# A weight matrix split into high and low halves by whole pieces, and the order of issue that goes with it

## The chip, the cores and the metric

The kernel runs on one core of a Trainium2 chip. The metric is the device time of one execution in microseconds (us). Five engines work in parallel, each on a queue of its own: TensorE (PE, matmuls, with PEld for the loads of its weights), VectorE (DVE), ScalarE (ACT), GpSimd (POOL) and SyncE (SP), which issues the DMAs. An engine takes the instructions of its queue in order; one that waits holds up all behind it.

## The reference

Three stages follow each other, in fp32: attention, an MLP with a leaky rectifier, and a gated MLP with an rms norm. The change is in the second, whose input x has 2304 rows (tokens) and whose weights are w_in[512, 2048] and w_out[2048, 512].

```python
def _moe_ref(x, w_in, w_out, alpha):
    h = x @ w_in
    g = np.maximum(h, 0.0) + alpha * np.minimum(h, 0.0)
    return (g @ w_out).astype(np.float32)

# around it: x is the attention's output (4 batches, 8 heads, 576 positions of 64:
# a softmax over a sequence averaged by 4, plus a softmax over |i - j| < 4), and
# the result goes through silu(n @ w_gate) * (n @ w_val) @ w_out2, n = rms norm of it
```

## The kernel before

TensorE multiplies 16-bit floats. To keep fp32 accuracy, each operand is split in two 16-bit halves, hi and lo, and a product is three matmuls (hi hi, hi lo, lo hi). The helper `split` does it in two instructions: ACT writes hi = f16(s * src), and DVE writes lo = f16(s * src - hi).

w_in comes from HBM in six pieces `p1`, of 384 columns each (the last of 128), since a piece fits in one tile: `load` issues the DMAs, `decode` turns the raw words (`wr`) into fp32 (`wc`) with ACT and DVE (L1186, L1189, L1191, L1194, L1195), and `square` sums squares on PE (`sqps`, L1207, read by DVE in L1208), from which a scale `swi` per piece is made (L430). Then `split_in` fills the tile `wi`, which holds both halves for 16 groups f of 128 hidden columns (each f: 512 numbers per partition and half, four blocks of 128 for the four slices of the contraction). It is called once per f, so three times for a piece.

`m1_first` is the first pass over x, in three chunks c of 192 tokens each. For c = 0 it goes over f in pairs: `split_in(f)`, `split_in(f + 1)`, then `h_mm`. `h_mm` makes 24 matmuls into a PSUM tile `hps` (L1432), ACT reads it with Relu into `g` (L1436), DVE adds the two sides of the rectifier in `hps` (L1438, one for each f), and `split` makes the halves of g (L439, L440; named `g` or `ghl`). The pool of `hps` has two buffers: a third pair must wait for the read-out of the first. `o_mm` (L1449) multiplies with w_out into `acc`. Around these, slots of other work are woven in: the attention of the next chunk (`lsps`, `dls`, `sps`, `dd`, `atps`, `lops`), and the pieces of later weights. The later weights `w`, among them those of the gated MLP, are split by whole pieces of 1536 numbers per partition. The gated MLP's own matmuls are those of L1684 (`pa`, `pb`, `pf`), read out by ACT in L1689 (`sn`), and its results leave through `ob`.

The order in which all these stand in the queues isn't that of the code. `issue_order` builds the graph of dependences, gives every instruction a duration from a formula, and schedules the list by "leads": the instruction with the largest lead that is ready goes first. It then adds a table `LEADS` of triples (from, to, shift), which shifts the lead of instructions by their number in the program; the queues that come out are fixed by added dependences. One instruction more or less in the program shifts the numbers behind it.

Of the kernel before, what the change touches and what calls it, by code (L numbers as in the profile page):

```python
# [18 lines left out]
def view(ap, dims, off=0, parts=None):  # L19
# [2 lines left out]


LEADS = (
# [43 lines left out]
)  # L68


# [249 lines left out]
def kernel(  # L320
# [14 lines left out]
    nc = tc.nc  # L335
    B, H, S, D = q.shape
    DM, FF = w_in.shape
    FF2 = w_gate.shape[1]
    KK = DM // 128
# [55 lines left out]
    wi = wts.tile([128, NF, 2, KK * 128], F16, name="wi")  # L395
# [3 lines left out]
    def col(i):  # L399
        return sc[:, i:i + 1]  # L400
# [37 lines left out]
    def split(hi, lo, src, s):  # L438
        nc.scalar.activation(out=hi, in_=src, func=AF.Copy, scale=s)  # L439
        nc.vector.scalar_tensor_tensor(out=lo, in0=src, scalar=s, in1=hi, op0=ALU.mult, op1=ALU.subtract)  # L440
# [686 lines left out]
    UC = 384  # L1127
    UW = KK * UC
# [3 lines left out]
    swi = const.tile([128, NP], F32, name="swi")  # L1132
# [78 lines left out]
    p1 = [Piece(w_in, f"u{i}", c0=i * UC, n=min(UC, FF - i * UC)) for i in range(6)]  # L1211
# [47 lines left out]
    def gcol(i, g):  # L1259
        return grp[:, i * NG + g:i * NG + g + 1]  # L1260
# [3 lines left out]
    def scale_out(g):  # L1264
# [12 lines left out]
        if g == NG - 1:  # L1277
# [3 lines left out]
            nc.vector.tensor_scalar(out=grp[:, 0:NG], in0=grp[:, 3 * NG:4 * NG], scalar1=col(S_WO),  # L1281
                                    scalar2=col(S_AL), op0=ALU.mult, op1=ALU.mult)

    def split_in(f):
        p = p1[f // 3]
        o = (f % 3) * 128
        c = p.cv()[:, :, o:o + 128]
        w = wi[:, f].rearrange("p a (k c) -> p a k c", k=KK)
        split(w[:, 0], w[:, 1], c, swi[:, f // 3:f // 3 + 1])

    def wo_f(f):
# [133 lines left out]
    def h_mm(x, f, c0, n, hl, first=False):  # L1425
        fs = hl.shape[1]
        ps = ps_w.tile([128, fs, n], F32, tag="w", name="hps")
        for j in range(fs):
            i = 0
            for kk in range(KK):  # L1430
                for a, b_ in ((0, 0), (0, 1), (1, 0)):
                    nc.tensor.matmul(ps[:, j], wi[:, f + j, a, kk * 128:(kk + 1) * 128], x[:, b_, kk, c0:c0 + n],  # L1432
                                     start=(i == 0), stop=(i == 3 * KK - 1))
                    i += 1
        g = wk.tile([128, fs, n], F32, tag="mm", name="g")
        nc.scalar.activation(out=g, in_=ps, func=AF.Relu, scale=-1.0)  # L1436
        for j in range(fs):
            nc.vector.scalar_tensor_tensor(out=ps[:, j], in0=g[:, j], scalar=oma[:, f + j:f + j + 1], in1=ps[:, j],  # L1438
                                           op0=ALU.mult, op1=ALU.add)
        if first or GF[f] == GF[f + fs - 1]:  # L1440
            split(hl[:, :, 0], hl[:, :, 1], ps, col(S_AL) if first else gcol(0, GF[f]))
            return
        for j in range(fs):
            split(hl[:, j, 0], hl[:, j, 1], ps[:, j], gcol(0, GF[f + j]))
# [53 lines left out]
    def m1_first(slots):  # L1498
# [12 lines left out]
        for c in range(3):  # L1511
            for f in range(0, NF, 2):
                if c == 0:
                    split_in(f)
                    split_in(f + 1)
                h_mm(xt(c // 2), f, c % 2 * CW, CW, hl(c, f, 2), True)
                slots[c](f, NF)
                slots[c](f + 1, NF)
# [513 lines left out]
    for i, (x, n) in enumerate(((al, NF), (rg, KK))):  # L2032
        ps = ps_t.tile([128, n], F32, tag="at", name="vecps")
# [98 lines left out]
```

## Time and profile before

| | |
|---|---|
| median of 3 runs | 911.7 us (911.51 to 911.85) |
| profiled execution | 912.48 us, of which the span 910.8 us |
| granted clock of PE, mean | 0.996 |
| PE busy | 885.3 us (97%) |
| DVE busy | 729.8 us (80%) |
| ACT busy | 570.0 us (63%) |
| POOL busy | 401.8 us (44%) |

The span runs from the first to the last instruction of the profiled execution; the 1.68 us around it are start and end. Busy time is the time in which an engine's instructions ran. A share over the whole span hides that stages differ: where PE has gaps is read in windows.

### The profile page before, as it was taken

To read this page: it belongs to the slowest core of one execution; us is meant where nothing else is said; L and a number is where in the kernel's file an instruction comes from. 1 tells how busy PE (TensorE), PEld (TensorE's weight loads), DVE (VectorE), ACT (ScalarE), POOL (GpSimd) and SP (SyncE) were. 2 spreads that over 40 slices of the span, in tenths; PEclk is the share of its full clock that TensorE was granted. 3 is DMA by queue.
4 is the path that set the end of the run, shared out by engine and by line. 5 is a ranking of instruction groups with operands and counts; after the bars stand their busy time and mean duration, and the time that the engine had idled before them with its cause. 6 is when DMAs were issued, how large, how long until landed. Compare 5 with 4: busy or idle time off the path is not lost.

```text
span 910.8 us, 16778 instructions
## 1 busy us (share of the span) xinstructions
PE 885.3 (97%) x6394; PEld 592.8 (65%) x6394; DVE 729.8 (80%) x1358; ACT 570.0 (63%) x1332; POOL 401.8 (44%) x314
## 2 busy tenths in 40 slices
PE   7987999999999999999999999999999999999997
PEld 5766877799866666666666656654566644556686
DVE  4789987799898788798789789999899891288772
ACT  5999986255763366765796688983366641356730
POOL 1100204999899999496201233211623100268630
PEclk9998999999999999999999999999999999999999
DMA  9976351174333141340630002220000001100001
GB/s 224 297 261 209 104 182 28 53 234 142 106 89 99 44 95 53 102 139 1 195 87 32 1 1 81 94 70 35 24 13 1 1 1 39 32 1 1 1 19 53
DMA packets 54111, 73.81 MB, mean 81 GB/s; under 512 B 22202, under 2 KB 35918, under 8 KB 54030
## 3 DMA queue, kind: packets, MB, share of 16 engines
q1 hardware_dynamic: 54030, 72.74, 26.7%
q8 instruction: 50, 0.82, 0.4%
q14 instruction: 31, 0.25, 0.1%
HBM read 68.01 MB, written 4.72 MB: 80 GB/s over the span
## 4 chain that ended last, share of the span: by engine, by line
PE 85%; ACT 6%; DVE 3%; DMA 2%; POOL 2%; issue 1%; SPq 0%; DVEq 0%; POOLq 0%; ACTq 0%
PE hps L1432 18%; PE acc L1449 17%; PE pa L1684 14%; PE oacc L1807 10%; PE pf L1684 7%; PE pb L1684 3%; PE px L1927 3%; POOL prod L599 1%; PE py L1927 1%; PE lsps L956 1%; PE tps L868 1%; ACT wr L1186 1%; PE lops L1012 1%; ACT wi L439 1%; PE ltps L1000 1%
## 5 line engine op out<-in xcount | busy, mean ns | idle before, releaser
L1432 PE MATMUL hps<-xt,wi 128*128 128x192 f16 (+1 forms) x1536 | 326.8, 290 | 4.6 <-DVE g L440 3.1
L1449 PE MATMUL acc<-ghl,wo 128*128 128x384 f16 (+1 forms) x960 | 231.0, 310 | 0.0
L1432 PEld LDWEIGHTS <-wi 128*128 128x128 f16 x1536 | 148.6, 100 | 57.1 <-issue 6.5
L1449 PEld LDWEIGHTS <-wo 128*128 128x128 f16 x1344 | 128.4, 98 | 56.7 <-issue 0.8
L545 POOL TENSOR_TENSOR prod<-cq,ckv 128x896 f32<-128x896 f32 x48 | 105.5, 2197 | 41.4 <-DVE hps L1438 35.3
L1684 PEld LDWEIGHTS <-ws 128*128 128x128 f16 x864 | 85.0, 99 | 56.7 <-issue 2.7
L599 POOL TENSOR_TENSOR prod<-ls,ckv 128x896 f32<-128x896 f32 x48 | 91.3, 1903 | 9.8 <-DVE lo L612 6.5
L1807 PE MATMUL oacc<-wi,wo 128*128 128x512 f16 x360 | 95.4, 379 | 0.2 <-ACT ob L1811 0.2
L1684 PEld LDWEIGHTS <-w 128*128 128x128 f16 x648 | 63.8, 99 | 41.6 <-issue 0.5
L1436 ACT ACTIVATE g<-hps 128x384 f32<-128x384 f32 x96 | 47.2, 492 | 61.5 <-PE hps L1432 60.9
L1438 DVE SCALAR_TENSOR_TENSOR hps<-g,oma,hps 128x192 f32<-128x192 f32 (+1 forms) x128 | 65.7, 515 | 18.3 <-ACT g L1436 17.3
L1449 PE MATMUL acc<-g,wo 128*128 128x384 f16 (+1 forms) x384 | 70.3, 286 | 0.1
L1664 POOL TENSOR_TENSOR ws<-w 128x768 f32<-128x768 f16 x12 | 22.1, 1852 | 106.8 <-DVE ws L1571 40.8
L1684 PE MATMUL pa<-x,w 128*128 128x384 f16 x216 | 67.1, 326 | 0.1
L1684 PE MATMUL pb<-x,w 128*128 128x384 f16 x216 | 66.2, 326 | 0.0
L1807 PEld LDWEIGHTS <-wo 128*128 128x128 f16 x360 | 35.3, 98 | 41.8 <-issue 0.5
L439 ACT ACTIVATE ghl<-hps,grp 128x384 f16<-128x384 f32 (+1 forms) x73 | 42.2, 578 | 31.9 <-DVE hps L1438 27.2
L612 DVE TENSOR_REDUCE lo<-prod 128x128 f32<-128x896 f32 x48 | 51.7, 1079 | 9.5 <-POOL prod L599 9.2
L1692 DVE TENSOR_TENSOR sn<-pf,sn 128x384 f32<-128x384 f32 x45 | 24.8, 552 | 42.6 <-ACT sn L1689 36.5
L556 DVE TENSOR_REDUCE ls<-prod 128x14 f32<-128x896 f32 x48 | 51.7, 1078 | 4.6 <-POOL prod L545 4.5
L1689 ACT ACTIVATE sn<-pa 128x384 f32<-128x384 f32 x66 | 31.9, 489 | 32.9 <-PE pa L1684 32.7
L1876 POOL TENSOR_TENSOR wr<-wi 128x512 f32<-128x512 f16 x12 | 15.1, 1261 | 84.1 <-DMA out_dram<-ob 77.5
(365 smaller groups left out, 2122.6 us busy)
## 6 DMA issues: line engine op xcount, KB each, us to landing
wr<-in_moe_w_out_dram SPq DMA_DIRECT2D x18, 512.0 KB
wr<-in_moe_w_in_dram SPq DMA_DIRECT2D x10, 768.0 KB
wr<-in_moe_w_gate_dram SPq DMA_DIRECT2D x8, 768.0 KB
wr<-in_moe_w_val_dram SPq DMA_DIRECT2D x8, 768.0 KB
ckv<-in_k_dram SPq DMA_DIRECT2D x7, 768.0 KB
ckv<-in_v_dram SPq DMA_DIRECT2D x7, 768.0 KB
wr<-in_moe_w_out_dram SPq DMA_DIRECT2D x20, 256.0 KB
out_dram<-ob SPq DMA_DIRECT2D x14, 256.0 KB
```

The costliest lines, as they stand in the source:

```text
L439: nc.scalar.activation(out=hi, in_=src, func=AF.Copy, scale=s)
L545: engs[i].tensor_tensor(out=pr, in0=view(st["q"][:, j, t:t + TP], [[D, TP], [0, ND], [1, D]]), in1=view(st["k"][:, j, t:t + TP], [[D, TP], ...
L556: nc.vector.tensor_reduce(out=st["s"][:, j, t:t + TP], in_=st.pop(("p", i)), axis=AX.X, op=ALU.add)
L599: engs[i].tensor_tensor(out=over(pr, i), in0=view(st["s"][:, j, t:t + TP], [[ND, TP], [1, ND], [0, D]]), in1=view(st["v"][:, j, t:t + TP], ...
L612: nc.vector.tensor_reduce(out=st["o"][:, t:t + TP, j], in_=view(pr, [[ND * D, TP], [ND, D], [1, ND]]), axis=AX.X, op=ALU.add)
L1432: nc.tensor.matmul(ps[:, j], wi[:, f + j, a, kk * 128:(kk + 1) * 128], x[:, b_, kk, c0:c0 + n], start=(i == 0), stop=(i == 3 * KK - 1))
L1436: nc.scalar.activation(out=g, in_=ps, func=AF.Relu, scale=-1.0)
L1438: nc.vector.scalar_tensor_tensor(out=ps[:, j], in0=g[:, j], scalar=oma[:, f + j:f + j + 1], in1=ps[:, j], op0=ALU.mult, op1=ALU.add)
L1449: nc.tensor.matmul(acc[e], wo_f(f)[:, a, e * 128:(e + 1) * 128], hl[:, b_], start=(f == f0 and i == 0), stop=(f == f1 and i == 2))
L1684: nc.tensor.matmul(ps, w[:, a, kk, c:c + 128], x[:, b_, kk], start=(start and n == 0), stop=(n == 3 * K2 - 1), skip_group_check=True)
L1807: nc.tensor.matmul(acc, uhl(f)[:, h, a, tt * 128:(tt + 1) * 128], w[:, b_, f % 3], start=(f == fs[0] and i == 0), stop=(f == fs[-1] and i ...
L1927: nc.tensor.matmul(ps, two(u[g])[:, a, tt * 128:(tt + 1) * 128], w(g, b_), start=(start and g == 0 and i == 0), stop=(g == F2 - 1 and i == 2),
```

## The change

w_in's halves are laid out by piece instead of by f: in the tile `wi` a piece has first all its hi numbers, then all its lo numbers, in the order of the decoded piece, so that one `split` can write a whole piece. `split_in` does that for f = 3, 6, 9 and 12 (1536 numbers per partition) and f = 15 (512, the last piece); for the other f above 2 it returns at once. f = 0, 1 and 2 are still split one by one, into the new layout. So 16 splits become 8, on ACT and on DVE. The matmuls read their weights through `wi_w`, again 128 columns in a row.

The program has 16 instructions less behind the splits, and the table of shifts is new: 1,385 triples in place of 212, which moves instructions in the queues of all engines.

```diff
 LEADS = (
-    (8102, 8103, 7000), (776, 777, -500), (3486, 3544, 1500), (7335, 7386, 500), (5591, 5593, -500),
...
 )
...
+    def wi_n(f):
+        return min(UC, FF - f // 3 * UC)
+
+    def wi_p(f):
+        o = f // 3 * 2 * UW
+        return wi.rearrange("p f a c -> p (f a c)")[:, o:o + 2 * KK * wi_n(f)].rearrange("p (a c) -> p a c", a=2)
+
+    def wi_w(f, a, kk):
+        o = kk * wi_n(f) + f % 3 * 128
+        return wi_p(f)[:, a, o:o + 128]
+
     def split_in(f):
+        if f > 2:
+            if f % 3 == 0:
+                w = wi_p(f)
+                split(w[:, 0], w[:, 1], p1[f // 3].c[:, 0:KK * wi_n(f)], swi[:, f // 3:f // 3 + 1])
+            return
         p = p1[f // 3]
         o = (f % 3) * 128
         c = p.cv()[:, :, o:o + 128]
-        w = wi[:, f].rearrange("p a (k c) -> p a k c", k=KK)
+        w = wi_p(f).rearrange("p a (k c) -> p a k c", k=KK)[:, :, :, o:o + 128]
         split(w[:, 0], w[:, 1], c, swi[:, f // 3:f // 3 + 1])
...
-                    nc.tensor.matmul(ps[:, j], wi[:, f + j, a, kk * 128:(kk + 1) * 128], x[:, b_, kk, c0:c0 + n],
+                    nc.tensor.matmul(ps[:, j], wi_w(f + j, a, kk), x[:, b_, kk, c0:c0 + n],
                                      start=(i == 0), stop=(i == 3 * KK - 1))
```

The order in the queues, at three places. Line numbers of after are 234 higher up to the helpers and 250 higher behind them: L673 and L674 are the two lines of `split`, L1686 and L1688 the read-out of `hps`, L1420 to L1429 the decode. First ACT's queue where the splits of `wi` begin, before:

```order
L439 ACTIVATE wi<-wc,swi 128x512 x5
L1186 ACTIVATE wr<-wr 128x768
L439 ACTIVATE wi<-wc,swi 128x512
L1189 ACTIVATE wr<-wr,nhalf 128x768
L1186 ACTIVATE wr<-wr 128x768
L439 ACTIVATE wi<-wc,swi 128x512 x2
L1436 ACTIVATE g<-hps 128x384
```

and after (128x4x128 are f = 0, 1 and 2 in this order, 128x1536 pieces 1 and 2):

```order
L673 ACTIVATE wi<-wc,swi 128x4x128
L673 ACTIVATE wi<-wc,swi 128x1536
L673 ACTIVATE wi<-wc,swi 128x4x128
L1420 ACTIVATE wr<-wr 128x768
L673 ACTIVATE wi<-wc,swi 128x1536
L1423 ACTIVATE wr<-wr,nhalf 128x768
L1420 ACTIVATE wr<-wr 128x768 x2
L1420 ACTIVATE wr<-wr 128x256
L1423 ACTIVATE wr<-wr,nhalf 128x768
L673 ACTIVATE wi<-wc,swi 128x4x128
```

Piece 1 now stands between f = 0 and f = 1, and f = 2 behind piece 2 and five steps of decode.

DVE's queue from the splits of `wi` to the first read-out of `hps`, before:

```order
L440 SCALAR_TENSOR_TENSOR wi<-wc,swi,wi 128x512 x4
L1195 SCALAR_TENSOR_TENSOR wc<-wr,wc 128x768
L440 SCALAR_TENSOR_TENSOR wi<-wc,swi,wi 128x512 x2
L1191 SCALAR_TENSOR_TENSOR wo<-wr 128x768
L1194 TENSOR_SCALAR wc<-wr 128x768
L440 SCALAR_TENSOR_TENSOR wi<-wc,swi,wi 128x512
L1195 SCALAR_TENSOR_TENSOR wc<-wr,wc 128x768
L1438 SCALAR_TENSOR_TENSOR hps<-g,oma,hps 128x192
L440 SCALAR_TENSOR_TENSOR wi<-wc,swi,wi 128x512
L1438 SCALAR_TENSOR_TENSOR hps<-g,oma,hps 128x192 x2
```

and after, from just ahead of the first read-out on (the 128x4x128 here is f = 2, `g_835` the halves of the first pairs):

```order
L1429 SCALAR_TENSOR_TENSOR wc<-wr,wc 128x768
L1429 SCALAR_TENSOR_TENSOR wc<-wr,wc 128x256
L1688 SCALAR_TENSOR_TENSOR hps<-g,oma,hps 128x192
L674 SCALAR_TENSOR_TENSOR wi<-wc,swi,wi 128x4x128
L1442 SCALAR_TENSOR_TENSOR sqps,s_111<-sqps,ident 128x128
L1688 SCALAR_TENSOR_TENSOR hps<-g,oma,hps 128x192
L1425 SCALAR_TENSOR_TENSOR wo<-wr 128x768
L1428 TENSOR_SCALAR wc<-wr 128x256
L674 SCALAR_TENSOR_TENSOR g_835<-hps,sc,g_835 128x2x192
```

The split of f = 2 moved from ahead of the first read-out to between its two steps.

ACT's queue at the first table load of the gated MLP (`sn`, `wi`, `uhl` and `wo` are here results read out of `pa`), before:

```order
L1200 ACTIVATE w_7141,s_115<-wc 128x1536
L1689 ACTIVATE sn<-pa 128x384
L1563 ACT_TABLE_LOAD
L1563 ACTIVATE th<-sn,gsc 128x384
L1689 ACTIVATE sn<-pa 128x384
L1473 ACTIVATE wi<-acc_6158,inv_106 128x192 x2
L1563 ACTIVATE th<-wi,gsc 128x384
L1689 ACTIVATE wo<-pa 128x384
```

and after:

```order
L1434 ACTIVATE w_7125,s_115<-wc 128x1536
L1939 ACTIVATE sn<-pa 128x384
L1939 ACTIVATE uhl<-pa 128x384
L1813 ACT_TABLE_LOAD
L1813 ACTIVATE th<-sn,gsc 128x384
L1939 ACTIVATE sn<-pa 128x384
L1939 ACTIVATE wo<-pa 128x384
```

`uhl` moved behind the sum of squares and so directly ahead of the load; the two steps of L1473 behind the second `sn` moved away.

## Rows read from the trace of the kernel before

**Rows 1.** The page: busy time of the engines, and the chain of work by engine.
```profile
PE 885.3 (97%) x6394; PEld 592.8 (65%) x6394; DVE 729.8 (80%) x1358; ACT 570.0 (63%) x1332; POOL 401.8 (44%) x314
...
PE 85%; ACT 6%; DVE 3%; DMA 2%; POOL 2%; issue 1%; SPq 0%; DVEq 0%; POOLq 0%; ACTq 0%
```

**Rows 2.** Windows of PE: start:end, length, busy (instructions), granted clock, DMA share, GB/s.
```profile
100.00:850.00 750.00, 746.27 (x5234) 1.00 0.21 65
850.00:911.00 61.00, 55.09 (x464) 0.99 0.08 27
```

**Rows 3.** Windows: length, busy of PE, PEld, DVE, ACT, POOL; clock, DMA share, GB/s.
```profile
60.00:70.00 10.00, 6.58 (x60) 5.54 (x61) 9.67 (x17) 9.67 (x16) 0.00 (x0) 1.00 0.93 337
70.00:80.00 10.00, 8.44 (x90) 7.59 (x90) 8.96 (x28) 10.00 (x25) 0.00 (x0) 0.83 0.79 249
80.00:90.00 10.00, 7.77 (x78) 7.00 (x76) 9.60 (x27) 10.00 (x31) 1.54 (x2) 0.83 0.57 153
90.00:100.00 10.00, 9.48 (x118) 7.37 (x117) 9.47 (x30) 7.79 (x28) 2.56 (x7) 1.00 0.45 124
```

**Rows 4.** Timeline, PE: start, length, engine, operation; in brackets idle before and releaser.
```profile
64.40 2.06 PE L1432 MATMUL hps<-xt,wi 128*128 128x192 f16 x23
...
71.15 0.96 PE L1432 MATMUL hps<-xt,wi 128*128 128x192 f16 x5 [3.07 <-DVE g L440]
```

**Rows 5.** Timeline of ACT (the first line) and of DVE, 58 to 71 us.
```profile
58.52 3.17 ACT L439 ACTIVATE wi<-wc,swi 128x512 f16<-128x512 f32 x5 [0.51 <-DVE swi L430]
...
59.34 2.73 DVE L440 SCALAR_TENSOR_TENSOR wi<-wc,swi,wi 128x512 f16<-128x512 f32 x4
...
62.85 1.41 DVE L440 SCALAR_TENSOR_TENSOR wi<-wc,swi,wi 128x512 f16<-128x512 f32 x2
...
68.41 0.98 DVE L1438 SCALAR_TENSOR_TENSOR hps<-g,oma,hps 128x192 f32<-128x192 f32 x2
...
70.49 0.61 DVE L440 SCALAR_TENSOR_TENSOR g<-hps,sc,g 128x384 f16<-128x384 f32 x1
```

**Rows 6.** Lines 439 and 440: count, min/median/max ns, first and last start, form.
```profile
L439 ACT ACTIVATE wi<-wc,swi x16: 704/715/766, 58.5 to 85.2; 128x512 f16<-128x512 f32 x16
...
L439 ACT ACTIVATE w<-wc,sw x8: 1566/1576/1667, 418.2 to 545.1; 128x1536 f16<-128x1536 f32 x8
...
L440 DVE SCALAR_TENSOR_TENSOR wi<-wc,swi,wi x16: 742/746/751, 59.3 to 86.4; 128x512 f16<-128x512 f32 x16
...
L440 DVE SCALAR_TENSOR_TENSOR w<-wc,sw,w x8: 1810/1816/1843, 421.8 to 546.7; 128x1536 f16<-128x1536 f32 x8
```

**Rows 7.** Windows of PE alone around its two holes, columns as in rows 2.
```profile
70.00:75.00 5.00, 3.81 (x30) 0.66 0.90 282
80.00:82.50 2.50, 0.60 (x9) 1.00 0.39 86
82.50:87.50 5.00, 4.67 (x43) 0.66 0.60 170
```

**Rows 8.** Waits of PE from 125 us on: us in total, times, longest.
```profile
PE pa L1684 <- ACT sn L1689: 1.6, 3, 0.8
PE atps L761 <- ACT dd L752: 1.0, 1, 1.0
PE sps L733 <- ACT qkT L723: 0.4, 1, 0.4
PE oacc L1807 <- ACT ob L1811: 0.2, 1, 0.2
PE hps L1432 <- DVE ghl L440: 0.2, 1, 0.2
```

**Rows 9.** Timeline of ACT, then of PE, at the table load.
```profile
526.87 1.28 ACT L1563 ACT_TABLE_LOAD   x1
...
529.20 0.97 PE L1684 MATMUL pa<-x,ws 128*128 128x384 f16 x5 [0.85 <-ACT sn L1689]
```

**Rows 10.** Timeline of DVE at the end.
```profile
905.53 0.47 DVE L1932 SCALAR_TENSOR_TENSOR ob<-px,sc,ob 128x256 f32<-128x256 f32 x1
```

319 rows, old and new, of the table LEADS are left out of this document.

## The prediction

> **What bounds the kernel now.** First the page: TensorE (PE) is busy in 885.3 us of a span of 910.8 us, and 85% of the chain that ended last is PE [rows 1]. So an edit on VectorE (DVE) or ScalarE (ACT) only counts where PE stands still. PE is idle for 25.5 us (910.8 - 885.3), and the next question is where. The two long windows say that between 100 and 850 us there are only 3.7 us of it (750 - 746.27), and that the last 61 us have 5.9, most of it behind the last matmul [rows 2]. In the windows of 10 us from 60 to 100 us the picture turns: PE has 6.58 us at 60 to 70, then 8.44, 7.77 and 9.48, while ACT has 9.67 and twice 10.00 and DVE 9 or more in all but one [rows 3]. So the stretch of 60 to 100 us is bound by the two engines that decode the weights of the first matrix product, split them and bring its results into SBUF; behind it PE is the bound. The longest wait of PE there is the 3.07 us of the third pair of `hps` for `g` [rows 4].
>
> What that wait is: `hps` has two PSUM buffers, so the third pair of hidden rows (f = 4, 5) can start only when the first pair is read out. The matmuls of pair two end at about 66.5 us (64.40 + 2.06), and pair three starts at 71.15, as soon as DVE's split of the first pair's `g` (70.49 + 0.61) is done [rows 4, 5]. The splits of `wi` stand among these on DVE and ACT, many of them back to back [rows 5].
>
> **The change part by part.** I take the profiled execution as the base: a span of 910.8 in 912.48 us, 1.68 us of it outside the span. It lies 0.78 above the median of 911.7, so what I work out as a difference is taken from the median.
>
> *Twelve splits become four.* On ACT and on DVE, pieces 1 to 4 (f = 3 to 14) lose three instructions of 128x512 each and get one of 128x1536; f = 0, 1, 2 and 15 stay. The wide form is in the trace already: 1576 ns on ACT and 1816 ns on DVE, in the splits of later weights, against 715 and 746 ns for the narrow one [rows 6]. By these medians a piece saves 3 x 715 - 1576 = 569 ns of ACT and 3 x 746 - 1816 = 422 ns of DVE. But neighbours overlap, so the durations overstate it: five narrow splits on ACT take 3.17 us, one every (3.17 - 0.715) / 4 = 0.614 us; four on DVE take 2.73, one every (2.73 - 0.746) / 3 = 0.661 us [rows 5]. With the same overlap, 0.10 and 0.085 us, taken from the wide one, a piece saves 3 x 0.614 - 1.476 = 0.37 us of ACT and 3 x 0.661 - 1.731 = 0.25 us of DVE. Four pieces: 1.5 us of ACT, 1.0 us of DVE. Ends: 0 (the saved time lies where PE is busy anyway) and 4 x 0.569 = 2.3 us. I take -1.0, DVE's, since DVE releases the longest wait.
>
> The Trainium skill, in "Perfetto Trace Analysis", section "Optimizing Scalar/DVE Operations", gives a fixed part of about 60 ns to a DVE and 93 ns to an ACT instruction on SBUF; by it eight fewer would save only some 0.5 and 0.7 us, an estimate from that page, and the sum would end 0.5 us higher. The spacings above hold for this kernel's form with its pointer operand, and they decide.
>
> *The halves laid out by piece.* A weight tile is still 128 columns in a row, and the number of matmuls and loads is unchanged: 0. The three narrow splits that remain write four runs of 128 columns instead of 512 in a row. They already read in such runs at 715 and 746 ns; I take 0, at most 3 x 0.05 us (some of ACT's spread, 704 to 766 [rows 6]).
>
> *The second pair comes later.* The order of issue shows it. On ACT, piece 1 is split as a whole between f = 0 and f = 1, and f = 2 comes after piece 2 and five decodes. On DVE, f = 2 stands directly ahead of the second `hps` step of the first pair, which began at 68.41 in the trace; before, its split was one of the two at 62.85 [rows 5]. So the matmuls of pair two, which now fill 2.0 us from 64.40 on (23 of 24 are in that row [rows 4]), move behind 68 us. Pair three still waits for the same read-out. Queued behind the late split of f = 2 on DVE are the second `hps` step and `g`, thus PSUM's buffer, thus pairs three to five. What absorbs it: at 80 to 82.5 PE has 0.60 of 2.5 us busy, so 1.9 us stand empty there [rows 7]. Ends 0 and +2.0 us; I take +0.6, nearer to 0 because of that hole.
>
> *The clock.* Behind the idle 3.07 us [rows 4] PE's granted clock is 0.66 in 70 to 75 us, and behind the hole at 80 to 82.5 it is 0.66 again in 82.5 to 87.5 [rows 7]: a mixture of 2.4 and 1.2 GHz. That is 0.34 x 5 = 1.7 us of full speed lost each time. With two holes before and, by the queues, two after, I take 0; one more or one fewer is worth 1.7.
>
> *A new table of shifts.* 212 triples become 1,385, so the queues of all engines differ from end to end. What can be won behind 100 us is bounded by the 3.7 us above; its waits are few: ACT `sn` 1.6 in three places, ACT `dd` 1.0, `qkT` 0.4, `ob` 0.2, DVE `ghl` 0.2 [rows 8]. For the two large ones I summed, with the durations of the trace, the work that stands ahead of waiter and releaser in either order. The matmul `atps` waits 1.0 us for a step on `dd`; in the new order PE has about 4 us more of other matmuls ahead of `atps`, ACT only 1.2 us more ahead of `dd`: closed. At 529.20 PE waits 0.85 us for an `sn` that stands behind a table load of 1.28 us [rows 9]; in the new order the load still stands there, but ACT has 2.2 us less ahead of that `sn`, PE only 0.3 us less: closed. The small ones of `qkT`, `ob` and `ghl` (0.8 together) close likewise; of the rest of `sn` (0.75) I give nothing, since ACT has as much more ahead there as PE. That is -1.0 - 0.85 - 0.6 = -2.4, with three quarters of the 0.8. Ends 0 and -3.7. New waits can arise elsewhere: the largest that such an order left is 1.0; I take +0.3, ends 0 and +2.0.
>
> *The tail.* SP's last two transfers of 256 KB now stand next to each other; before, transfers of the other kind lay between. The last row's sums are ready with a DVE step of 0.47 us at 905.53 [rows 10]. I take +0.2, ends 0 and +0.5 (one such step).
>
> Sum: -1.0 + 0.6 + 0 - 2.4 + 0.3 + 0.2 = -2.3 us, so 911.7 - 2.3 = **909.4 us**. Own range from 907.5 to 910.6.
>
> **The rivals.** *No change.* The new order has as many waits behind 100 us as the old, and the late second pair costs PE 1.0 us, half of its work, as much as the splits give back; with the tail 911.7 - 1.0 + 1.0 + 0.2 = 911.9. For it: 3.7 us in 750 is already little. Against it: both large waits have lost their cause in the order.
>
> *Slower.* Whole pieces are too coarse. In the queues the read-outs of pairs three to five stand 2.7, 3.9 and 4.0 us of DVE work later than before, because local attention of the next chunk was drawn ahead of them. If PE has nothing to put there, the chain of two buffers passes the last delay on: +4.0 - 1.0, and a third low-clock stretch +1.7, of which the closed waits give back 2.4: 911.7 + 2.3 = 914.0. It decides from the point where pair three starts after about 75 us instead of 71.15 and PE is busy in less than the 22.8 us of 60 to 90 [rows 3]. The same section of the Trainium skill says that where Scalar and Vector aren't saturated but cause bubbles elsewhere, breaking instructions up can get work done sooner. By that rule this is the likely way; here both engines are saturated (9 to 10 of 10 us), which weakens it.
>
> *All waits go.* The order also closes the remaining waits (-3.7) and one of the two holes with its low clock (-1.7), and ACT's 1.5 us count in place of 1.0, with 1.0 for the late pair and tail: 911.7 - 3.7 - 1.7 - 1.5 + 1.0 = 905.8.
>
> **How the numbers follow.** Forecast 0.51, no change 0.14, slower 0.19, all waits 0.16. Some 0.2% (1.8 us) is what a measurement here can tell from no change, so faster means below 909.9 and slower above 913.5. Of the forecast's 0.51, about 0.37 lie below 909.9 and 0.14 above. Faster 0.37 + 0.16 = 0.53, same 0.14 + 0.14 = 0.28, slower 0.19. The range reaches into the two outer rivals until some 0.08 is left out below and 0.12 above: 906.0 to 914.0.
>
> **What would show it.** The wide splits on `wi` at about 1576 and 1816 ns, four each, else the first term is wrong. Pair three's start: at 71 +- 1.5 us the forecast holds, at 75 the slower rival. PE busy in 60 to 100: 33 us or more supports the first terms (32.3 now). PE idle between 100 and 850: about 1.5 us if the fourth term is right, 3.7 if not; no wait of `atps` for `dd` and none for the `sn` behind the table load. The prediction is wrong if PE's idle time behind 100 us grows, or if the low clock spreads beyond 70 to 90 us.

## The result, and the profile after

The changed kernel takes 916.8 us in the median of 5 runs (916.0 to 919.5) against 911.85 of the kernel before; the ratio is 1.0051, with a 95% interval of 1.0026 to 1.0076. Measured again on another chip, with 12 runs against 35 of the kernel before, it is 917.6 against 915.1 us, a ratio of 1.0031 (1.0014 to 1.0047). So it is slower, by some 2.5 to 5 us, where 2.3 us less were forecast. The runs of the kernel before spread widely there, from 910.9 to 920.8, and its first runs were among its fastest; the comparisons below are therefore made on one chip, or as ratios.

The rows that answer to [rows 1 to 3], of the changed kernel, with a profiled execution of 918.19 us and a span of 916.5; first the page:

```profile
PE 885.1 (97%) x6394; PEld 590.7 (64%) x6394; DVE 718.3 (78%) x1350; ACT 565.5 (62%) x1324; POOL 403.6 (44%) x314
```

PE has the same 6394 matmuls and is busy for 885.1 us, as long as before, in a span 5.7 us longer. DVE has 11.5 us less of busy time and ACT 4.5; of that the splits make 1.7 and 2.3 us by the medians of [rows 6]. The rest wasn't followed up. The windows of 10 us, then two long ones (PE alone), show where PE stands:

```profile
60.00:70.00 10.00, 5.32 (x41) 3.91 (x40) 9.78 (x15) 10.00 (x13) 0.00 (x0) 0.63 0.89 276
70.00:80.00 10.00, 8.46 (x88) 7.52 (x87) 8.61 (x27) 10.00 (x27) 1.69 (x2) 0.86 0.83 248
80.00:90.00 10.00, 7.84 (x70) 6.54 (x71) 9.75 (x24) 9.56 (x30) 1.10 (x2) 0.66 0.59 148
90.00:100.00 10.00, 10.00 (x127) 8.66 (x125) 7.55 (x23) 6.04 (x22) 0.98 (x5) 1.00 0.42 114
```

```profile
100.00:850.00 750.00, 742.82 (x5220) 1.00 0.22 65
850.00:917.00 67.00, 60.72 (x498) 0.99 0.08 25
```

In 60 to 100 us PE is busy for 31.6 us (32.3 before), and its clock is low in three windows, 0.63, 0.86 and 0.66, not in two. Between 100 and 850 us it is idle for 7.2 us, not 3.7 [rows 2]. The clock was forecast to cost nothing more, and the idle time behind 100 us to shrink; both have grown.

The first holes, on PE's timeline (start, length, idle before):

```profile
59.79 0.34 PE L1682 MATMUL hps<-xt,wi 128*128 128x192 f16 x2 [1.18 <-ACT wi L673]
60.70 0.26 PE L1682 MATMUL hps<-xt,wi 128*128 128x192 f16 x1 [0.57 <-DVE wi L674]
61.56 0.46 PE L1441 MATMUL sqps<-wc 128*128 128x128 bf16 x5 [0.61 <-DVE wc L1429]
...
63.96 1.78 PE L1682 MATMUL hps<-xt,wi 128*128 128x192 f16 x10 [0.70 <-DVE wi L674]
68.41 0.50 PE L1682 MATMUL hps<-xt,wi 128*128 128x192 f16 x2 [2.67 <-ACT wi L673]
...
80.99 0.58 PE L1441 MATMUL sqps<-wo 128*128 128x128 bf16 x7 [1.95 <-DVE wo L1425]
...
84.57 0.32 PE L1682 MATMUL hps<-xt,wi 128*128 128x192 f16 x1 [0.62 <-DMA sd<-in_k_dram]
```

The first pair starts with f = 0 and then waits for f = 1, which stands behind the wide split of piece 1; the second pair waits 2.67 us for f = 2, as the order said. What that does to the clock, in windows of PE (granted clock behind the busy time):

```profile
57.00:60.00 3.00, 1.37 (x18) 1.00 0.89 311
60.00:62.50 2.50, 1.32 (x17) 1.00 0.92 280
62.50:72.50 10.00, 6.50 (x43) 0.50 0.90 292
82.50:90.00 7.50, 6.88 (x60) 0.54 0.63 159
```

PE was busy 2.69 of the 5.5 us from 57 to 62.5; then its clock is 0.50 for 10 us, the lower level, though it is busy for 6.5 of them. Before, it had 1.98 and 2.10 us in the first two windows and a clock of 0.90 over the third:

```profile
57.00:60.00 3.00, 1.98 (x15) 1.00 0.66 225
60.00:62.50 2.50, 2.10 (x13) 1.00 0.89 297
62.50:72.50 10.00, 5.83 (x59) 0.90 0.92 328
```

The waits of PE from 125 us on, for [rows 8]:

```profile
PE hps L1682 <- DVE ghl L674: 1.9, 2, 1.5
PE pa L1934 <- ACT sn L1939: 1.0, 2, 0.6
PE pa L1934 <- DVE th L1950: 0.8, 1, 0.8
PE atps L995 <- ACT dd L986: 0.5, 1, 0.5
PE pa L1934 <- ACT wi L1939: 0.4, 1, 0.4
PE qkps L954 <- POOL prod L779: 0.3, 1, 0.3
PE vqps L905 <- DMA sd<-in_v_dram: 0.2, 1, 0.2
```

The `sn` behind the table load no longer makes PE wait, and `dd` half as long as before. In their place stand `ghl`, `th` and `wi`, which PE did not wait for before or only for 0.2 us. Together the waits of this list are 5.1 us, those of [rows 8] 3.4.

### The profile page after: what moved, and what is told of

The parts are those of the page before. It is cut to its first block, busy times and chain, and to the rows that moved or that the text cites. A ratio compares the mean times of both kernels' runs of the same rounds, so it can differ in the third digit from the quotient of the medians.

```text
span 916.5 us, 16743 instructions
## 1 busy us (share of the span) xinstructions
PE 885.1 (97%) x6394; PEld 590.7 (64%) x6394; DVE 718.3 (78%) x1350; ACT 565.5 (62%) x1324; POOL 403.6 (44%) x314
## 4 chain that ended last, share of the span: by engine, by line
PE 77%; ACT 7%; DMA 5%; DVE 4%; POOL 4%; issue 1%; SPq 1%; DVEq 0%; POOLq 0%; ACTq 0%
PE hps L1682 16%; PE acc L1699 16%; PE pa L1934 13%; PE oacc L2057 10%; PE pf L1934 6%; PE px L2177 3%; PE pb L1934 3%; POOL prod L779 2%; PE py L2177 1%; ACT wr L1420 1%; DMA sd<-in_v_dram 1%; ACT wr L1423 1%; PE lsps L1190 1%; ACT wi L673 1%; PE lops L1246 1%
## 5 line engine op out<-in xcount | busy, mean ns | idle before, releaser
L1682 PE MATMUL hps<-xt,wi 128*128 128x192 f16 (+1 forms) x1536 | 321.5, 290 | 8.1 <-ACT wi L673 3.8
L1699 PE MATMUL acc<-ghl,wo 128*128 128x384 f16 (+1 forms) x960 | 224.9, 310 | 0.0
L1688 DVE SCALAR_TENSOR_TENSOR hps<-g,oma,hps 128x192 f32<-128x192 f32 (+1 forms) x128 | 65.6, 517 | 31.6 <-ACT g L1686 30.6
L1686 ACT ACTIVATE g<-hps 128x384 f32<-128x384 f32 x96 | 46.6, 489 | 65.0 <-PE hps L1682 65.0
L1699 PE MATMUL acc<-g,wo 128*128 128x384 f16 (+1 forms) x384 | 73.7, 286 | 0.0
L1934 PE MATMUL pa<-x,w 128*128 128x384 f16 x216 | 64.8, 326 | 0.8 <-DVE th L1950 0.8
L673 ACT ACTIVATE ghl<-hps,grp 128x384 f16<-128x384 f32 (+1 forms) x73 | 41.9, 574 | 25.8 <-DVE hps L1688 22.2
L674 DVE SCALAR_TENSOR_TENSOR ghl<-hps,grp,ghl 128x384 f16<-128x384 f32 (+1 forms) x73 | 44.1, 606 | 11.7 <-ACT ghl L673 11.1
L1914 POOL TENSOR_TENSOR wo<-w 128x768 f32<-128x768 f16 x17 | 32.0, 1890 | 42.6 <-DVE ws L1821 26.3
```

What stands on the lines that cost most here:

```text
L1682: nc.tensor.matmul(ps[:, j], wi_w(f + j, a, kk), x[:, b_, kk, c0:c0 + n], start=(i == 0), stop=(i == 3 * KK - 1))
L1699: nc.tensor.matmul(acc[e], wo_f(f)[:, a, e * 128:(e + 1) * 128], hl[:, b_], start=(f == f0 and i == 0), stop=(f == f1 and i == 2))
L1914: nc.gpsimd.tensor_tensor(out=tmp(t), in0=w[:, 0], in1=w[:, 1], op=ALU.add)
L1934: nc.tensor.matmul(ps, w[:, a, kk, c:c + 128], x[:, b_, kk], start=(start and n == 0), stop=(n == 3 * K2 - 1), skip_group_check=True)
```

## The experiments

Two things changed together: the splits, and the order of all queues. In the experiments the order is written into the kernel as a list per engine, in place of the scheduler's result, so that either can be had alone. Line numbers differ from kernel to kernel; the tiles tell what a row is.

```diff
-    end, seq, d = run(preds, succs, lead, True, dur)
-    best = max(end), seq, lead
+    seq = json.loads(zlib.decompress(base64.b64decode(ORDER)))
+    best = 0.0, seq, None
```

**Splits and order apart.** Four kernels on one chip (before: 913.4 us in the median of 27).

The wide splits in the old order, and the narrow ones in the new:

> The splits by whole pieces, with every queue in the order of the kernel before: a wide split stands where the first of its three narrow ones stood, nothing else moves. Theory 1, the new order costs the time and the splits save what their spacing says: 1.0 to 1.5 us less than the kernel before, about 910.5 to 911. Theory 2, a whole piece is too coarse a step by itself: some 4 to 5 us more than before, about 916. The pair f = 4, 5 starts near 71 us by theory 1, after 74 by theory 2.

Measured: 916.3 us, ratio 1.0026 (1.0006 to 1.0045). The time is that of theory 2, and in its profile the pair f = 4, 5 starts at 74.51 us, also as theory 2 said. But of the 3.4 us that this is later than before, 2.35 arise ahead of the first split of `wi` (60.87 against 58.52 us), where the two kernels issue the same; the sign doesn't decide.

> The kernel before with its 16 narrow splits, but every queue in the order of the changed kernel: three narrow splits stand in a row where a wide one stood. Theory 1 (order): as slow as the changed kernel or up to 1.5 us slower, 917 to 918.5. Theory 2 (coarse splits): back near 912.

Measured: 918.4 us, ratio 1.0049 (1.0034 to 1.0063). The new order costs with the old splits as well, as theory 1 said. But the wide splits in the old order save nothing either; they are slower, if by less. In the profile of the wide splits in the old order the clock is low too, 0.52 in the window of 60 to 70 us (0.63 in the changed kernel):

```profile
60.00:70.00 10.00, 7.18 (x52) 0.52 0.91 320
```

The orders of the two stretches, exchanged:

> The wide splits, with the order of before for all instructions that it places before about 118 us, and the new order for the rest. In the trace of the changed kernel PE has lost 1.1 us more than before by 120 us and 5.4 us by the end. If the order behind 118 us costs by itself: about 4 us more than the kernel before, 915 to 916. If those later gaps are only a late start handed on: about 911. Theory 2 gives 916 for another reason and is told apart by the kernel with the old order throughout.

Measured: 921.2 us, ratio 1.0085 (1.0061 to 1.0109), 7.8 us more than the kernel before and not the 4 expected. A part of it belongs to the joint: in the window of 118 to 150 us PE is busy for 30.05 of 32 us (30.62 in the changed kernel), and its clock, 1.00 there in the changed kernel, is 0.95.

> The wide splits, with the new order for all that it places before about 118 us and the order of before for the rest. If the order of the first 118 us costs (f = 2 late, PE idle and then at 1.2 GHz): 1 to 2 us more than the kernel before, about 913. If only the order behind it costs: 911 to 912.

Measured: 916.8 us, ratio 1.0028 (1.0006 to 1.0050). The new order behind 118 us costs where it follows the old head: from 1.0026 to 1.0085. Behind the new head the old order gave no clear gain, 1.0028 against the 1.0031 to 1.0051 of the changed kernel, on other chips, and 3 us more than the 913 expected; the joint at 118 us brought a wait of its own there (2.3 us of PE for `outd`).

**The late second pair.** Moved: f = 1 and f = 2 directly behind f = 0, on ACT and DVE.

```diff
-[f0] [piece 1] [f1] ... [piece 2] ... [f2]
+[f0] [f1] [f2] [piece 1] ... [piece 2] ...
```

> The changed kernel and its order, but on ACT and DVE the splits of f = 1 and f = 2 stand directly behind that of f = 0, ahead of the wide splits of pieces 1 and 2. If the late second pair is what costs in the first 118 us: PE no longer waits 2.67 us for the split of f = 2, and the time falls by 2 to 3 us against the changed kernel, to about 914. If it only costs where PE would have waited later anyway: within 1 us of the changed kernel.

Measured: 917.8 us, ratio 1.0026 (1.0010 to 1.0041), against 1.0051 and 1.0031 of the changed kernel on two other chips: the intervals overlap, and the 2 to 3 us aren't shown. The wait for f = 2 is gone, and PE waits for the next thing that DVE has to decode, 1.85 and 1.91 us:

```profile
PE sqps L1407 <- DVE wc L1395: 3.8, 2, 1.9
```

and its clock is low as before, 0.55 over 60 to 67.5 and 0.54 over 70 to 77.5 us:

```profile
60.00:67.50 7.50, 4.96 (x32) 0.55 0.65 218
70.00:77.50 7.50, 6.53 (x50) 0.54 0.90 295
```

The hole moved, and the low clock stayed. So to have the pair early, with the rest of the order as it is, doesn't bring the time back.

**The clock.** Added: matmuls whose result is overwritten, in the holes. They need only x, which is there early, and write the PSUM tile that the waiting matmuls will start afresh.

```diff
+        if first and c0 == 0 and x is xt(0):
+            for _ in range(FILL.get(f, 0)):
+                nc.tensor.matmul(ps[:, 0], x[:, 0, 0, 0:128], x[:, 0, 0, 0:n], start=True, stop=True)
         for j in range(fs):
...
+FILL = {0: 10, 2: 30}
```

> The changed kernel and its order, with 40 matmuls of 192 columns more on PE whose results are overwritten: 10 ahead of the first pair and 30 ahead of the second, in the time in which PE waits for wi. They take no split away. If PE's low clock behind these holes costs (6.5 us of busy time times clock lost between 55 and 100 us, against 3.0 in the kernel before): granted clock near 1.0 in 60 to 75 us and 2 to 3 us less than the changed kernel, about 914. If DVE and ACT set the pace of the stretch whatever PE's clock: the clock is higher and the time the same, 916 to 917.5.

Measured: 915.1 us, ratio 0.9992 (0.9976 to 1.0007), beside the 917.8 us of the kernel with the early pair on the same chip. Then beside the changed kernel itself:

> The changed kernel itself, on the same chip as the three kernels beside it, which differ from it by one thing each. By its first measurement 1.005 of the kernel before; the runs of the kernel before spread by 8 us and its profile had a lucky clock, so 1.002 to 1.005 here.

> The changed kernel with the 40 filling matmuls, again, beside the changed kernel. If PE's clock behind the holes of 58 to 68 us costs: 2 to 3.5 us less than the changed kernel. If the difference seen before came from the chip: within 1 us of it.

Measured on one chip: 917.6 us (1.0031, from 1.0014 to 1.0047) and, with the filling, 915.6 us (1.0011, from 0.9993 to 1.0029): 2.0 us less, with 40 matmuls more (95% interval 0.3 to 3.0 us, from the runs of the two). The mean clock over the span rises from 0.988 to 0.995 in the profiled executions, and from 0.991 to 0.995 in the mean of the twelve. In the windows of 62.5 to 72.5 and 82.5 to 90 us it is 0.50 and 0.65 without the filling:

```profile
62.50:72.50 10.00, 7.20 (x49) 0.50 0.88 289
82.50:90.00 7.50, 7.16 (x72) 0.65 0.64 177
```

and 0.87 and 0.79 with it:

```profile
62.50:72.50 10.00, 7.88 (x78) 0.87 0.86 286
82.50:90.00 7.50, 7.50 (x81) 0.79 0.59 161
```

So the low clock in the stretch of 60 to 100 us costs the changed kernel about 2 us. Does it cost the kernel before too? There the filling stands ahead of the first pair and in the two holes of 1.1 and 3.1 us (the second is that of [rows 4]), in the PSUM tile of the next piece's squares:

> The kernel before with 77 matmuls more whose results are overwritten, in three holes of PE: 9 of 192 columns ahead of the first pair, 18 and 50 of 128 columns into the next piece's sqps tile, in the holes of 1.1 and 3.1 us at 66 to 71 us. If the low clock behind these holes costs: 1 to 3 us less than the kernel before. If DVE and ACT set the pace: the same time.

> The kernel before with the 77 filling matmuls, again, since its first profile was disturbed. If the low clock costs the kernel before as it costs the changed one: 1 to 2 us less than the kernel before, 0.998 to 0.999, with granted clock near 1.0 in 60 to 80 us. If the filling only helps where the holes are the changed kernel's: 0.9995 to 1.001.

Measured: 915.8 us, ratio 1.0006 (0.9986 to 1.0026), and on another chip 916.3 us, ratio 1.0010 (0.9991 to 1.0029). No gain, though the clock is 1.00 throughout 60 to 100 us in the second one's profile. So the price of the low clock is the changed kernel's own. In the one profile of the kernel before, the clock is low for less time, within 70 to 75 and 82.5 to 87.5 us [rows 7]; that this is the reason isn't shown.

**The order behind 118 us, with the clock held up.** Two kernels more on the chip of the changed kernel's 917.6 us:

> As the changed kernel with the filling matmuls, but all that the new order places behind about 118 us stands in the order of before. In the traces the new order loses about 1.9 us more at 120 to 150, 2.4 more at 360 to 390 and 1.2 more at 570 to 600, and 0.8 to 2 less at 210 to 270 and 510 to 540: some 3 us net. If that is a cost of the order: 2 to 4 us less than with the new order and the same filling. If these gaps only move: within 1 us.

Measured: 914.0 us, ratio 0.9985 (0.9963 to 1.0007): 1.7 us less than with the new order behind 118 us (95% interval 0.5 to 3.4, from the runs of the two), a little under the 2 to 4 expected. Windows of PE, first of the kernel with the filling and the new order, then of the one with the old:

```profile
350.00:400.00 50.00, 46.95 (x321) 1.00 0.31 96
570.00:600.00 30.00, 28.20 (x178) 1.00 0.33 106
```

```profile
350.00:400.00 50.00, 49.93 (x344) 1.00 0.31 96
400.00:450.00 50.00, 47.70 (x301) 1.00 0.28 83
570.00:600.00 30.00, 29.27 (x184) 1.00 0.32 106
```

At 350 to 400 us the new order leaves PE 3.1 us idle and the old 0.1; at 570 to 600 us 1.8 and 0.7. These belong to the new order: the changed kernel has 47.98 and 28.22 us busy there, the narrow splits in the new order 48.13 and 28.20. But the old order isn't free of such waits: at 400 to 450 us it loses 2.3 us here, to the same kind of wait for `ghl`, and nothing in another profile of the same kernel (the second run below, 50.00 busy). Over 118 to 850 us PE is idle for 6.5 us with the new order, and for 5.4 and 4.0 in the two profiles with the old. The first of the two gaps, in the changed kernel, on the timeline of DVE, ACT and PE:

```profile
361.77 0.57 ACT L673 ACTIVATE ghl<-hps,grp 128x384 f16<-128x384 f32 x1
361.82 1.07 DVE L790 TENSOR_REDUCE ls<-prod 128x14 f32<-128x896 f32 x1
362.81 0.60 DVE L674 SCALAR_TENSOR_TENSOR ghl<-hps,grp,ghl 128x384 f16<-128x384 f32 x1
...
363.47 0.81 PE L1682 MATMUL hps<-xt,wi 128*128 128x384 f16 x4 [1.53 <-DVE ghl L674]
```

DVE takes a reduction of 1.07 us of the local attention first, and `ghl`, whose hi half ACT has ready at 362.34, only then. With it `hps` is free, for which PE has been waiting 1.53 us. No instruction is slow here; the one that frees the buffer stands behind other work in DVE's queue. In the kernel before, PE has no idle time in 350 to 400 us:

```profile
350.00:400.00 50.00, 50.00 (x344) 1.00 0.29 93
```

**What the wide splits save.** The same order and the same filling with narrow splits, on the same chip:

> The new order throughout and the same 40 filling matmuls, but 16 narrow splits, three in a row where a wide one stood. It tells what the wide splits save by themselves, with the clock held up. By their spacing on DVE and ACT: 1.0 to 1.5 us more than with the wide ones. If PE's end hides it: the same within 0.5 us.

Measured: 916.7 us, ratio 1.0019 (1.0001 to 1.0037), against 915.6 with the wide ones. The 1.0 us has the size that the spacing on DVE gave, but it isn't clear of noise: from the runs of the two its 95% interval is -0.7 to 1.9.

**Where the wide split stands.** In the old order, with the wide split at the place of the last of its three narrow ones:

> The wide splits with the order of before, each wide split where the last of its three narrow ones stood, not the first. If the early place of the wide split (ahead of a read-out of hps) made the 2.4 us of the kernel with the old order: back to the kernel before or 1 us under it. If the wide step itself costs, or if the 2.4 us were PE's clock alone: 915 to 916.5.

Measured: 915.1 us, ratio 1.0008 (0.9986 to 1.0030): as the kernel before. Against the 1.0026 of the early place, on another chip, the difference is inside the intervals: whether the place matters can't be told.

**The late read-out.** In the changed kernel the fourth pair starts at 84.57 us, 9.7 us later than before, because ACT and DVE make the halves of the second pair's g only behind the wide splits of pieces 3 and 4 (DVE at 83.9). Moved: those halves ahead of the two wide splits, and on PE the fourth pair ahead of the squares that wait at 81 us.

```diff
-[piece 3] ... [piece 4] ... [g of pair 2]
+[g of pair 2] [piece 3] ... [piece 4]
```

> The changed kernel and its order with one thing moved: the halves of the second pair's g are made on ACT and DVE ahead of the wide splits of pieces 3 and 4, not behind them, and PE's matmuls of the fourth pair (f = 6, 7) stand ahead of the rest of the sqps that waits at 81 us. In the trace of the changed kernel that pair starts at 84.6 us, 9.7 later than before. If a read-out queued behind two wide splits costs: the pair starts near 79 us, PE's hole at 79 to 81 and the low clock behind it go, and the time falls by 1.5 to 3 us against the changed kernel, to 1.000 to 1.0015 of the kernel before. If it is only moved work: within 1 us of the changed kernel, 1.003.

Measured: 920.6 us, ratio 1.0060 (1.0037 to 1.0083), no gain against the changed kernel.

> Filling matmuls and the old order behind 118 us, again, as the base for the kernel with the early g on the same chip: 0.9985 of the kernel before as measured, between 0.997 and 1.000.

> The same, with the 40 filling matmuls and the old order behind 118 us. If the three costs found add (low clock behind the first holes 2.0, order behind 118 us 1.7, the late read-out 1.5 to 3): 1.5 to 3 us less than the kernel beside it that lacks only the early g, about 0.996 of the kernel before. If the head is paced by ACT and DVE as a whole: no less than that kernel.

Measured: 913.3 us, ratio 0.9998 (0.9983 to 1.0014), and with the early g 916.8 us, ratio 1.0023 (1.0007 to 1.0039). The time is 3.5 us longer, not shorter, though the fourth pair does start earlier, at 79.42 us in the profile of the first of the two kernels; the hole now follows it:

```profile
79.42 2.15 PE L1648 MATMUL hps<-xt,wi 128*128 128x192 f16 x24
82.68 0.58 PE L1407 MATMUL sqps<-wo 128*128 128x128 bf16 x7 [1.12 <-DVE wo L1391]
```

So moving the read-out forward gains nothing, and that theory falls. With the filling and the early g, PE is busy for 5.54 us of 80 to 90, without the early g for 7.65: the work done ahead of 81 us is missing behind it. Of the 3.5 us, 2.3 are the wait for `ghl` at 400 to 450 us, which the profile with the early g has and the one without hasn't; as the first profile without it has this wait too, it isn't shown that the early g brings it.

## Why the prediction was wrong, point by point

*What bounds the kernel* was right: PE's busy time is unchanged, and the difference lies where PE stands still or runs slowly.

*Twelve splits become four.* In the trace the wide splits on `wi` stand four times on either engine, in their group with the narrow ones (min/median/max ns):

```profile
L673 ACT ACTIVATE wi<-wc,swi x8: 705/1162/1625, 59.0 to 82.8; 128x512 f16<-128x512 f32 x4, 128x1536 f16<-128x1536 f32 x4
L674 DVE SCALAR_TENSOR_TENSOR wi<-wc,swi,wi x8: 743/1278/1909, 59.9 to 85.4; 128x512 f16<-128x512 f32 x4, 128x1536 f16<-128x1536 f32 x4
```

The longest are 1625 and 1909 ns against the 1576 and 1816 taken; the new writes in four runs of 128 columns cost nothing (f = 0, 1 and 2 take 705 to 722 on ACT and 743 to 747 on DVE). The term of -1.0 us has the size that the narrow splits with the filling gave against the wide ones, +1.0, but that difference may be anything from -0.7 to 1.9: the term isn't refuted, and whether the spacing of neighbours or the durations (1.7 us on DVE) were the right reading isn't shown. The estimate from the Trainium skill's fixed parts ("Perfetto Trace Analysis", section "Optimizing Scalar/DVE Operations"), 0.5 us, isn't excluded either.

*The second pair comes later.* It did, by about 4 us (68.41), and pair three still began in time (near 72 us, 71.15 before). The term of +0.6 isn't refuted: with the pair moved back the ratio is 1.0026, 0.5 us under the 1.0031 of the changed kernel's second measurement, but on another chip and with other waits in its place.

*The clock* is the first step that failed. "With two holes before and, by the queues, two after, I take 0" counted holes, and left out how the idle time lies in front of them and how long the clock stays low behind them. The new order breaks up the start of the first pair as well: 1.18, 0.57, 0.61 and 0.70 us of idle time within 5 us. No single one is long, but the clock is at 0.50 for 10 us behind them, and at 0.54 in the 7.5 us from 82.5 on. By the prediction's own measure that is 0.50 x 10 + 0.46 x 7.5 = 8.5 us of full speed lost, against 2 x 1.7 = 3.4 before. Of these 5 us more, the filling gave back 2.0, near the 1.7 that the prediction had put on "one more".

*A new table of shifts* is the second step that failed, and in size the larger: -2.4 + 0.3 was put in. The waits that were looked at went nearly as said: `dd` from 1.0 to 0.5, the `sn` behind the table load gone, `qkT` and `ob` gone behind 125 us. But the new order has others, which could be seen only by looking at all of the waits it makes, not at those it removes: `ghl` 1.9, `th` 0.8, `wi` 0.4, and one for `qkT` of 1.2 just ahead of 125 us. PE's idle time between 100 and 850 us is 7.2 us, so by this profile the term is about +3.5 and not -2.1; by experiment, with the clock held up, going back to the old order behind 118 us gave 1.7 us. The end of +2.0 for new waits was too near, since nothing in the traces bounded it: it came from the longest wait that a well-fitted order had left, and a new order need not be one. Both signs of being wrong that the prediction had named came true: the idle time behind 100 us grew, from 3.7 to 7.2, and the low clock spread beyond 70 to 90 us, from 62.5 on.

*The tail* of +0.2 fits: the last window has 5.7 us of idle time inside the span before (60.8 - 55.09) and 5.8 after (66.5 - 60.72).

*The rivals.* The slower one gave 914.0 us, by a chain of late read-outs. It had the sign, not the mechanism: pair three began near 72 us, not after 75, and the kernel with the early g shows that an earlier read-out of the second pair doesn't help. Its condition on PE (busy in less than 22.8 us of 60 to 90) came true in the first profile, at 21.6, and not in the second, at 23.0. Narrow splits in the same order were no faster, 1.0049 and 1.0019. The rule of the Trainium skill beside this rival ("Perfetto Trace Analysis", section "Optimizing Scalar/DVE Operations"), that smaller instructions can get work done sooner, is for engines that aren't saturated. ACT and DVE are busy for 8.6 to 10 us of each 10 from 60 to 90 us here, so these runs don't test it.

What adds up, on one chip: the changed kernel is 2.5 us slower than before (917.6 - 915.1). With the clock held up it is 0.6 slower (915.6), with the old order behind 118 us too it is 1.1 us faster (914.0; ratio 0.9985, from 0.9963 to 1.0007; on a second chip 0.9998). That kernel has the wide splits and equals the kernel before within 0.2%. No version that was run beats it clearly.

A third thing lay in the base. The prediction's trace of the kernel before begins its splits of `wi` at 58.52 us [rows 5]; other profiles of the old order begin them at up to 63.63, as the last section shows, and the twelve profiles with the new order up to there at 58.5 to 60.2. So the time of the kernel before holds a part that varies by some 5 us ahead of the first split, and 911.7, under the later medians of 913.4 to 915.3, was a lucky draw. From the first split to the end, the profile before takes 852.3 us (910.8 - 58.5), the changed kernel 857.5 (916.5 - 59.0) and 856.2 in its second profile: behind that point, by these single profiles, the change costs 4 to 5 us, more than the 2.5 of the medians.

Open is why the wide splits in the old order are 2.4 us slower by their ratio. Counted from the first split, their profiles take 853.6 us, and 853.2 with the late place, some 1 us more than before. The low clock of the one profile isn't the reason: of the twelve runs, the eight with a mean clock of 0.996 or more have a median of 916.7 us, no less than the whole. Open, too, is why the early g costs.

## What to carry to other kernels

Where an edit comes with a new order of issue, the edit's own saving can be the smaller part: here some 1 us, not clear of noise, against the 2.0 and 1.7 us that clock and order cost. Such an order is to be judged by all the waits that it makes on the engine that bounds, not by whether it removes the ones the old trace shows. And where several short holes stand in a row on TensorE, as here four of 0.57 to 1.18 us, the granted clock behind them is worth a look; matmuls with a result that nobody reads, put into the holes, show what it costs. They gave 2.0 us in the changed kernel and nothing in the kernel before.

## What the runs showed of the hardware that was not expected

The granted clock stayed at 0.50, that is 1.2 GHz of 2.4, for a whole 10 us (62.5 to 72.5) though PE was busy for 6.50 of them, and for 7.20 in the second profile. The Trainium skill, in "TensorE: Matmul & The Clock Gate", Part 1, gives these two as the levels of the engine's clock gate. The windows agree, with 0.50 and 1.00 wherever they don't hold a change.

Also, runs of one kernel differ by up to 10 us on a chip: the kernel before from 910.9 to 920.8. A part of it arises ahead of 60 us. The kernels of the old order issue the same instructions in the same order up to the first split of `wi`, and it starts at 58.52 us in the profile of the kernel before [rows 5], but up to 5 us later in those of the wide splits in the old order, at the early and at the late place, and of the filled kernel before (from the top; L639 and L646 are the ACT line of `split` there):

```profile
60.87 2.79 ACT L639 ACTIVATE wi<-wc,swi 128x512 f16<-128x512 f32 x3
63.44 2.80 ACT L639 ACTIVATE wi<-wc,swi 128x512 f16<-128x512 f32 x3
63.63 2.56 ACT L646 ACTIVATE wi<-wc,swi 128x512 f16<-128x512 f32 x4 [0.51 <-DVE swi L637]
```

What delays it wasn't followed up. Another part is the wait for `ghl` at 400 to 450 us, 2.3 us in one profile of the kernel with the filling and the old order behind 118 us, and 0 in the other.
